# One product per chunk for dV and the transpose of P, in a backward pass of two attention blocks

## The chip, the cores and the metric

The kernel runs on one core of a Trainium2 chip. The metric is the device time of one execution in microseconds, and the median of three runs counts. The profile is of one further execution, taken by the hardware profiler.

## The reference

Two independent attention blocks, A and B, read caches of keys and values. Each has an input x of 8 batches x 96 tokens x 640, 32 heads of width 128, and 512 cached keys and values per batch and head. The reference returns the forward output of both and the gradients of all ten inputs, in bfloat16:

```
q = (x @ wq) per head;  scores = q k^T * 128^-0.5;  P = softmax(scores)
O = P v;  out = concat_heads(O) @ wo;  result = concat(out_A, out_B)
then the gradients of x, k_cache, v_cache, wq, wo for a given grad_out
```

Per head and batch (a "chunk" below: 64 heads x 8 batches = 512 of them) the backward pass needs dV = P^T dO, dP = dO V^T, delta = the row sums of O * dO, dS = (dP - delta) * P, dK = dS^T Q and dQ = dS K.

## The kernel before

An emitter collects pieces of code with a tick and a slot and writes them out in that order; one tick starts one chunk, and each stage of a chunk has a tick of its own (`OFF`). The tile framework then schedules the instructions of each engine by its own costs, hands out buffers and sets the semaphores. So eight chunks are in flight, and in a tick PE goes, after the head work of the tick before, through:

- S = Q K^T of the chunk that is 3 ticks old (L301, 96x512); DVE takes the negative row maximum `negm` (L303), ACT the exponential with its row sums (L313), DVE the reciprocal `rinv` (L323), POOL the scaling to `P_sb` (L332);
- `c_s8`: the dQ product of the oldest chunk (L343) and the four transposes of dS (L349), which DVE copies to `dST_sb` (L351); `c_s7`: dK (L435), evacuated by ACT (L438);
- `c_s45`: the O product (L362) and the four transposes of P (L368, P as the stationary operand and a 96-column identity as the moving one). O^T, dQ^T and P^T share one PSUM bank, `x_ps`; ACT evacuates O^T and dQ^T together to `OD` (L378) and then P^T to `PT_sb` (L381), which the O product of the next tick reads;
- `c_s4`: dV (L392, the same stationary chunks of P with 128 columns of dO as the moving operand) in a bank of its own, `dV_ps`, evacuated by ACT (L395);
- `c_s6`: dP (L420) in a bank, and the delta sum (L422), a product of `prod` with a column of ones, in another bank, `dl_ps`. `prod` = O * dO is POOL's work (L410). DVE computes `dS_sb` from both banks and `P_sb` (L424).

Around these lies the work per head and per group of heads: projections (L246), transposes of Q and dO to token-major form in `pD` (L261; the copies of both, `Qnat_h` and `dOnat_h`, are DVE's, L163), the products for dwo and dwq (L472, L493), and out and dx (L517). All products take their bank from one pool of eight, `ps`, in turn:

```
        def bank(shape, dt, name):
            return ps.tile(shape, dt, name=name, tag="bank")
```

The order in which the pieces of a tick are written, by slot: S, then `c_s8`, `c_s7`, `c_s45` (slot S5), `c_s4` (S4), `c_s6` (S6), and the head and group work. Loads, transposing loads and stores are DMAs on SP's queue.

Of the kernel before, what the change touches and what calls it, by code (L numbers as in the profile page):

```python
# [7 lines left out]
ACT = mybir.ActivationFunctionType  # L8
ALU = mybir.AluOpType
AX = mybir.AxisListType  # L10
F32 = mybir.dt.float32
BF16 = mybir.dt.bfloat16
PSUM = bass.MemoryType.PSUM
# [33 lines left out]
OFF = dict(ldk=-5, ldv=-4, kt=-3, vt=0, s2=3, s3=3, s4=4, s5=5, s6=6, s7=7, s8=8)  # L47
HK = dict(pA=-10, pA2=-9, pB=-3, pC0=[-2, 0], pC1=[-1, 0], pD1=1, pD0=2, qA0=18, qA1=17, qA1e=21, qDw=(18, 29), qB=[19, 20], qD=[(18, 0, 2), (19, 2, 4), (21, 4, 5)])
EV = dict(pB0="act", pB1="dve", pC00="act", pC01="act", pC10="act", pC11="dve", pD0="dve", pD1="dve", qA0="act", qA1="dve", qB0="act", qB1="dve", qD="dve", gU="act")
# [4 lines left out]
SLOTS = dict(LOAD=0, S2A=5, S2B=5.5, S1=6, S8=10, S7=20, S5=30, S4=40, S6=50, S3A=52, S3B=53, S5B=54, HEAD=SL_HEAD, GRP=SL_GRP)  # L54


def build_block(tc, em, tick0, blk, x, kc, vc, wq, wo, g_all, out_all, dx, dk, dv, dwq, dwo, ident, ones, pools, HG=6, first=True, groups=None):
    nc = tc.nc
    B, Sq, D = x.shape
    _, H, Sk, Dh = kc.shape  # L60
# [5 lines left out]
    KC = Sk // 128  # L66
    NB = 2
    assert B % NB == 0 and H % 2 == 0
    scale = float(Dh) ** -0.5
# [9 lines left out]
    while t0 < T:  # L79
        w = 512 if T - t0 >= 512 else (256 if T - t0 >= 256 else (128 if T - t0 >= 128 else T - t0))  # L80
# [4 lines left out]
    while c0 < D:  # L85
        w = 512 if D - c0 >= 512 else (256 if D - c0 >= 256 else 128)
# [12 lines left out]
    const, ps, kvp, wk, hd, hst, grp = (pools[k] for k in ("const", "ps", "kvp", "wk", "hd", "hst", "grp"))  # L99

    def bank(shape, dt, name):
        return ps.tile(shape, dt, name=name, tag="bank")
# [3 lines left out]
    SB = {}  # L106
    HS = pools["HS"]
    CS = pools["CS"]
# [49 lines left out]
    def evac(eng, dst, src, sc=None):  # L158
        if eng == "act":
            nc.scalar.activation(dst, src, ACT.Identity, scale=(1.0 if sc is None else sc))  # L160
        else:
            if sc is None:
                nc.vector.tensor_copy(dst, src)  # L163
            else:
                nc.vector.tensor_scalar(dst, src, float(sc), None, op0=ALU.mult)
# [84 lines left out]
    def pD(h, which):  # L250
        def f():
            st = HS[(blk, h)]
            src = st["QT_h"] if which == 0 else st["dOT_h"]
            dst = hd.tile([Sq, B * 128], BF16, name="Qnat_h" if which == 0 else "dOnat_h")
            st["Qnat_h" if which == 0 else "dOnat_h"] = dst
            for b0 in range(0, B, 8):
                nb = min(8, B - b0)
                n_ps = bank([Sq, 8 * 128], BF16, "n_ps")
                for i in range(nb):
                    b = b0 + i  # L260
                    nc.tensor.transpose(n_ps[:, i * 128:(i + 1) * 128], src[:, b * Sq:(b + 1) * Sq], ident[:])  # L261
                evac(EV["pD%d" % which], dst[:, b0 * 128:(b0 + nb) * 128], n_ps[:, 0:nb * 128])
        return f

    def c_ld(h, b, n, bufs):
# [89 lines left out]
    def c_s45(tick, k8, k5, k4):  # L355
        def f():
            pt_ps = XP.pop(tick)
            if k5 is not None:
                st = CS[(k5[0], k5[1], k5[2])]
                OT_ps = pt_ps[:, 0:2 * Sq].bitcast(F32)  # L360
                for c in range(KC):
                    nc.tensor.matmul(OT_ps, st["V_sb"][:, c, :], st["PT_sb"][:, c * Sq:(c + 1) * Sq], start=(c == 0), stop=(c == KC - 1))  # L362
            if k4 is not None:
                st4 = CS[(k4[0], k4[1], k4[2])]
                P_sb = st4["P_sb"]
                PT_ps = pt_ps[:, 4 * Sq:4 * Sq + KC * Sq]
                for c in range(KC):
                    nc.tensor.transpose(PT_ps[:, c * Sq:(c + 1) * Sq], P_sb[:, c * 128:(c + 1) * 128], ident[0:Sq, 0:Sq])  # L368
            both = [(k, which) for which, k in enumerate((k5, k8)) if k is not None]
            if both:  # L370
                at = [(HS[(k[0], k[1])]["slot"], k[2] * Sq) for k, _ in both]
                v = OD[:, both[0][1], at[0][0], at[0][1]:at[0][1] + Sq]
                src = pt_ps[:, 2 * Sq * both[0][1]:2 * Sq * (both[-1][1] + 1)].bitcast(F32)
                if len(both) == 2:
                    step = (OD.shape[2] + at[1][0] - at[0][0]) * T + at[1][1] - at[0][1]
                    v = bass.AP(v.tensor, v.offset, [v.ap[0], (step, 2), (1, Sq)])
                    src = src.rearrange("p (a q) -> p a q", a=2)
                nc.scalar.activation(v, src, ACT.Identity, scale=1.0)  # L378
            if k4 is not None:
                PT_sb = wk.tile([128, KC * Sq], BF16, name="PT_sb", bufs=2)  # L380
                nc.scalar.activation(PT_sb[:], PT_ps, ACT.Identity, scale=1.0)  # L381
                st4["PT_sb"] = PT_sb
        return f

    def c_s4(h, b):
        def f():
            st = CS[(blk, h, b)]
            hs = HS[(blk, h)]
            P_sb = st["P_sb"]
            dV_ps = bank([128, KC * 128], F32, "dV_ps")  # L390
            for c in range(KC):
                nc.tensor.matmul(dV_ps[:, c * 128:(c + 1) * 128], P_sb[:, c * 128:(c + 1) * 128], hs["dOnat_h"][:, b * 128:(b + 1) * 128], start=True, stop=True)  # L392
            if b % 2 == 0:
                SB[(blk, h, b // 2, "v")] = wk.tile([128, 2, KC * 128], BF16, name="dV_sb", bufs=4)
            nc.scalar.activation(SB[(blk, h, b // 2, "v")][:, b % 2], dV_ps[:], ACT.Identity, scale=1.0)  # L395
        return f

    def c_st(h, b, which):
# [5 lines left out]
    def c_s5b(h, b):  # L404
# [6 lines left out]
            st["prod"] = prod  # L411
        return f

    def c_s6(h, b):
        def f():
            st = CS[(blk, h, b)]
            hs = HS[(blk, h)]
            tok = slice(b * Sq, (b + 1) * Sq)
            dP_ps = bank([Sq, Sk], F32, "dP_ps")
            nc.tensor.matmul(dP_ps[:], hs["dOT_h"][:, tok], st["VT"], start=True, stop=True)  # L420
            dl_ps = bank([Sq, 1], F32, "dl_ps")
            nc.tensor.matmul(dl_ps[:], st["prod"][:], ones[:, 0:1], start=True, stop=True)  # L422
            dS_sb = wk.tile([Sq, Sk], BF16, name="dS_sb", bufs=2)
            nc.vector.scalar_tensor_tensor(dS_sb[:], dP_ps[:], dl_ps[:, 0:1], st["P_sb"][:], op0=ALU.subtract, op1=ALU.mult)  # L424
            st["dS_sb"] = dS_sb
        return f
# [136 lines left out]
    for g in range(NG):  # L563
        h0 = GH0[g]
        for hh in range(groups[g]):
            h = h0 + hh
# [16 lines left out]
            for b in range(B):  # L583
                ct = c0t + b
                if b % NB == 0:
                    em.add(tick0 - 12 if first and h == 0 and b == 0 else ct + OFF["ldk"], SLOTS["LOAD"], c_ld(h, b, "K", 7))
                    em.add(ct + OFF["ldv"], SLOTS["LOAD"], c_ld(h, b, "V", 6))
                    if not k_on_pe(h, b):
                        em.add(ct + OFF["kt"], SLOTS["LOAD"] + 1, c_xt(h, b, "KT", 4))
                    em.add(ct + OFF["vt"], SLOTS["LOAD"] + 1, c_xt(h, b, "VT", 4))  # L590
                if k_on_pe(h, b):
                    em.add(ct + 2, SLOTS["S1"], c_s1(h, b), pe=223)
                em.add(ct + OFF["s2"], SLOTS["S2A"], c_s2a(h, b))
                em.add(ct + OFF["s2"], SLOTS["S2B"], c_s2b(h, b))
                em.add(ct + OFF["s3"], SLOTS["S3A"], c_s3a(h, b))
                em.add(ct + OFF["s3"], SLOTS["S3B"], c_s3b(h, b))
                em.add(ct + OFF["s5"], SLOTS["S5B"], c_s5b(h, b))
                if b % 2 == 1:
                    em.add(ct + OFF["s4"] + 1, SLOTS["LOAD"] + 1.5, c_st(h, b, "v"))
                    em.add(ct + OFF["s7"] + 1, SLOTS["LOAD"] + 1.5, c_st(h, b, "k"))  # L600
                em.add(ct + OFF["s4"], SLOTS["S4"], c_s4(h, b))
                for i, o in enumerate(("s8", "s7", "s5", "s4")):
                    SX.setdefault(ct + OFF[o], [None] * 4)[i] = (blk, h, b)
                em.add(ct + OFF["s6"], SLOTS["S6"], c_s6(h, b))
                em.add(ct + OFF["s7"], SLOTS["S7"], c_s7(h, b))
            hk = HK if first or h < H - 1 else dict(HK, qA0=13, qB=[14, 15], qA1=16, qD=[(19, 0, 2), (19, 2, 4), (19, 4, 5)])
# [42 lines left out]
def _kernel_impl(tc, A_x, A_k_cache, A_v_cache, A_wq, A_wo, B_x, B_k_cache, B_v_cache, B_wq, B_wo, grad_out,  # L649
           out_0, out_1, out_2, out_3, out_4, out_5, out_6, out_7, out_8, out_9, out_10, HG=5, slots=None, off=None, hk=None, ev=None, gspread=None, groupsA=None, groupsB=(5, 5, 5, 5, 5, 5, 2)):  # L650
    global GSPREAD0, GSPREAD1
    nc = tc.nc
# [10 lines left out]
    with ExitStack() as ctx:  # L663
        P = lambda **kw: ctx.enter_context(tc.tile_pool(**kw))
        cst = P(name="gconst", bufs=1)
        ident = cst.tile([128, 128], BF16, name="ident")
# [4 lines left out]
        nc.vector.memset(warm[:], 1.0)  # L671
        pools = dict(
            const=P(name="const", bufs=1),
            ps=P(name="ps", bufs=8, space=PSUM),
            kvp=P(name="kv", bufs=11),
            wk=P(name="wk", bufs=3),
            hd=P(name="hd", bufs=2),
# [7 lines left out]
        pools["SX"] = {}  # L685
        pools["XP"] = {}
        pools["OD"] = pools["const"].tile([128, 2, HG + 2, A_x.shape[0] * A_x.shape[1]], BF16, name="OD", bufs=1)
        pools["HS"] = {}
        pools["CS"] = {}
        em = Emitter()  # L690
# [77 lines left out]
```

## Time and profile before

| | |
|---|---|
| time, median of three runs | 1630.79 us (1629.3 to 1632.03) |
| the profiled execution | 1629.74 us, span 1628.0 us |
| granted TensorE clock | 0.999 |
| DMA | 454.96 MB, mean 279 GB/s |

In a row of the profile's groups the line is that of the kernel above, then come engine, operation, what is written and read with shapes and count; behind the first bar the busy time in us and the mean of one in ns; behind the second the engine's idle time just before them, in us, and what ended it. In the waits a row reads: engine and work that waited, what it waited for, us in total, times, longest us. In the timeline a row gives start and duration in us; several equal instructions in a row are one line, with their count. Products overlap: the duration of one is its latency, and the distance between starts is what it costs PE.

### The profile page before, as it was taken

What the parts mean: (1) busy time and instruction counts of PE and PEld (TensorE: products, weight loads), DVE (VectorE), ACT (ScalarE), POOL (GpSimd) and SP (SyncE); (2) the same over time, 40 slices, a digit from 0 to 9 for tenths busy, and PEclk for the clock granted to TensorE, in tenths of its full rate; (3) what the DMA queues carried; (4) which work ended last, traced back from release to release, by engine and by line L of the source; (5) the groups of instructions that cost most, each with busy time, mean ns of one, the idle gap of its engine ahead of it and who ended that gap; (6) DMA issues with size and microseconds to landing.
All of it is one profiled execution on the core that took longest, in us unless ns stands there. A gap on an engine that the chain in (4) does not pass through costs nothing.

```text
span 1628.0 us, 55048 instructions
## 1 busy us (share of the span) xinstructions
PE 1605.0 (99%) x20881; PEld 1286.4 (79%) x21048; DVE 1269.9 (78%) x2907; ACT 1391.5 (85%) x3518; POOL 528.5 (32%) x1034
## 2 busy tenths in 40 slices
PE   8999999999999999999999999999999999999998
PEld 7887787787788787877878777877877877877876
DVE  6886687778788788788878767878878878777887
ACT  7999898798898797988879889978987977987984
POOL 2333333233333233333323323323333333332332
PEclk9999999999999999999999999999999999999999
DMA  9999999999999999999999999999999999999994
GB/s 268 284 290 293 274 292 285 278 275 289 283 281 287 274 282 278 272 277 299 277 303 287 285 285 286 283 294 277 276 295 268 294 288 266 283 274 285 287 280 142
DMA packets 875626, 454.96 MB, mean 279 GB/s; under 512 B 548192, under 2 KB 875360, under 8 KB 875360
## 3 DMA queue, kind: packets, MB, share of 16 engines
q1 hardware_dynamic: 875360, 451.43, 112.8%
q8 instruction: 165, 2.70, 0.7%
q14 instruction: 101, 0.83, 0.1%
HBM read 161.09 MB, written 159.12 MB: 197 GB/s over the span
## 4 chain that ended last, share of the span: by engine, by line
PE 93%; DVE 2%; ACT 2%; issue 1%; DMA 1%; SPq 0%; POOL 0%; DVEq 0%; ACTq 0%; POOLq 0%
PE q_ps L246 13%; PE o_ps L517 12%; PE dK_ps L435 7%; PE dV_ps L392 7%; PE dP_ps L420 7%; PE S_ps L301 7%; PE dwo_ps L472 6%; PE dwq_ps L493 6%; PE dst_ps L349 5%; PE x_ps L368 5%; PE x_ps L362 5%; PE x_ps L343 5%; PE n_ps L261 3%; PE nat_ps L458 3%; PE woT_ps L213 1%
## 5 line engine op out<-in xcount | busy, mean ns | idle before, releaser
L332 POOL TENSOR_SCALAR P_sb<-E_sb,rinv 96x512 bf16<-96x512 bf16 x512 | 354.2, 692 | 1072.2 <-DVE rinv L323 1038.4
L313 ACT ACTIVATE E_sb<-S_ps,negm 96x512 bf16<-96x512 f32 x512 | 356.3, 696 | 117.2 <-DVE negm L303 111.7
L424 DVE SCALAR_TENSOR_TENSOR dS_sb<-dP_ps,dl_ps,P_sb 96x512 bf16<-96x512 f32 x512 | 382.8, 748 | 43.6 <-PE dl_ps L422 36.6
L438 ACT ACTIVATE dK_sb<-dK_ps 128x512 bf16<-128x512 f32 x512 | 307.4, 600 | 84.8 <-PE dK_ps L435 83.8
L303 DVE TENSOR_REDUCE negm<-S_ps 96x1 f32<-96x512 f32 x512 | 347.6, 679 | 37.5 <-PE S_ps L301 36.4
L395 ACT ACTIVATE dV_sb<-dV_ps 128x512 bf16<-128x512 f32 x512 | 316.2, 618 | 0.0
L381 ACT ACTIVATE PT_sb<-x_ps 128x384 bf16<-128x384 bf16 x512 | 258.1, 504 | 0.0
L517 PEld LDWEIGHTS <-OD 128*128 128x128 bf16 x1536 | 135.3, 98 | 102.8 <-issue 2.0
L392 PE MATMUL dV_ps<-dOnat_h,P_sb 96*128 96x128 bf16 x2048 | 197.9, 219 | 0.6 <-DVE dOnat_h L163 0.6
L435 PE MATMUL dK_ps<-Qnat_h,dS_sb 96*128 96x128 bf16 x2048 | 198.0, 219 | 0.0
L420 PE MATMUL dP_ps<-VT,dOT_h 128*96 128x512 bf16 x512 | 195.3, 381 | 0.3
L323 DVE RECIPROCAL rinv<-rowsum 96x1 f32<-96x1 f32 x512 | 80.3, 157 | 144.8 <-ACT E_sb L313 141.5
L351 DVE COPY dST_sb<-dst_ps 128x384 bf16<-128x384 bf16 x512 | 177.7, 347 | 17.5 <-PE dst_ps L349 17.5
L410 POOL TENSOR_TENSOR prod<-OD,dOT_h 128x96 bf16<-128x96 bf16 x512 | 186.5, 364 | 8.8 <-ACT OD L378 8.2
L301 PE MATMUL S_ps<-KT,QT_h 128*96 128x512 bf16 x488 | 184.9, 379 | 0.4
L378 ACT ACTIVATE OD<-x_ps 128x192 bf16<-128x192 f32 (+1 forms) x515 | 173.3, 336 | 3.7 <-PE x_ps L343 3.7
L349 PE MATMUL dst_ps<-ident,dS_sb 96*128 96x96 bf16 x2048 | 172.4, 206 | 0.5 <-ACT PT_sb L381 0.3
L362 PE MATMUL x_ps<-PT_sb,V_sb 128*128 128x96 bf16 x2048 | 172.2, 206 | 0.2 <-ACT PT_sb L381 0.2
L368 PE MATMUL x_ps<-ident,P_sb 96*128 96x96 bf16 x2048 | 171.9, 205 | 0.6 <-POOL P_sb L332 0.3
L343 PE MATMUL x_ps<-dST_sb,K_sb 128*128 128x96 bf16 x2048 | 170.9, 206 | 0.0
L343 PEld LDWEIGHTS <-K_sb 128*128 128x128 bf16 x2048 | 135.3, 98 | 38.2
L493 PE MATMUL dwq_ps<-dQnat,x_nat 128*128 128x256 bf16 x960 | 142.7, 273 | 0.0
(75 smaller groups left out, 3042.5 us busy)
## 6 DMA issues: line engine op xcount, KB each, us to landing
out_dram<-dV_sb SPq DMA_DIRECT2D x256, 256.0 KB, 3.6
out_dram<-dK_sb SPq DMA_DIRECT2D x256, 256.0 KB, 3.5
K_sb<-in_A_k_cache_dram SPq DMA_DIRECT2D x128, 256.0 KB, 4.1
V_sb<-in_A_v_cache_dram SPq DMA_DIRECT2D x128, 256.0 KB, 3.9
K_sb<-in_B_k_cache_dram SPq DMA_DIRECT2D x128, 256.0 KB, 4.0
V_sb<-in_B_v_cache_dram SPq DMA_DIRECT2D x128, 256.0 KB, 4.0
out_dram<-dwo_sb SPq DMA_DIRECT2D x64, 160.0 KB, 3.2
out_dram<-dwq_sb SPq DMA_DIRECT2D x32, 320.0 KB, 4.2
```

What stands on the lines that cost most here:

```text
L301: nc.tensor.matmul(S_ps[:], hs["QT_h"][:, tok], st["KT"], start=True, stop=True)
L303: nc.vector.tensor_reduce(negm[:], S_ps[:], axis=AX.X, op=ALU.max, negate=True)
L313: nc.scalar.activation(E_sb[:], st["S_ps"][:], ACT.Exp, bias=st["negm"][:], scale=1.0, accum_out=rowsum[:])
L332: pinned(nc.gpsimd.tensor_scalar(P_sb[:], st["E_sb"][:], st["rinv"][:], 0.0, op0=ALU.mult, op1=ALU.add))
L343: nc.tensor.matmul(dQT_ps, st["K_sb"][:, c, :], st["dST_sb"][:, c * Sq:(c + 1) * Sq], start=(c == 0), stop=(c == KC - 1))
L392: nc.tensor.matmul(dV_ps[:, c * 128:(c + 1) * 128], P_sb[:, c * 128:(c + 1) * 128], hs["dOnat_h"][:, b * 128:(b + 1) * 128], start=True, s ...
L395: nc.scalar.activation(SB[(blk, h, b // 2, "v")][:, b % 2], dV_ps[:], ACT.Identity, scale=1.0)
L420: nc.tensor.matmul(dP_ps[:], hs["dOT_h"][:, tok], st["VT"], start=True, stop=True)
L424: nc.vector.scalar_tensor_tensor(dS_sb[:], dP_ps[:], dl_ps[:, 0:1], st["P_sb"][:], op0=ALU.subtract, op1=ALU.mult)
L435: nc.tensor.matmul(dK_ps[:, c * 128:(c + 1) * 128], dS_sb[:, c * 128:(c + 1) * 128], hs["Qnat_h"][:, b * 128:(b + 1) * 128], start=True, s ...
L438: nc.scalar.activation(SB[(blk, h, b // 2, "k")][:, b % 2], dK_ps[:], ACT.Identity, scale=1.0)
L517: nc.tensor.matmul(o_ps[:], src[:, t * 128:(t + 1) * 128], rhs, start=(hh == 0), stop=(hh == groups[g] - 1))
```

## The change

The four transposes of P and the four dV products of a chunk become four products with the same stationary chunk of P and 224 moving columns: 128 of dO and a 96-column identity, side by side. For this the token-major dO lies in a constant tile `DN`, double buffered by head, in which each pair of batches shares one identity: dO, identity, dO. The identities are written once at the start. The result goes into a pair of PSUM banks, `wide`, of a pool of its own with one buffer; two chunks of 224 f32 columns lie in each bank. ACT evacuates P^T (now f32) and then dV from it. The delta sum, `c_dl`, is issued just before that product, and goes to the last column of the second bank of the same tick's pair. The pool of single banks shrinks from eight to six.

```diff
@@ pD @@
+            if which == 0:
+                dst = hd.tile([Sq, B * 128], BF16, name="Qnat_h")
+                st["Qnat_h"] = dst
+            else:
+                dst = st["DN_h"] = pools["DN"][:, (blk * H + h) % 2]
...
+                    v = dst[:, b0 // 2, 0:128]
+                    v = bass.AP(v.tensor, v.offset, [v.ap[0], (128 * 2 + Sq, nb // 2), (128 + Sq, 2), (1, 128)])
+                    evac(EV["pD1"], v, n_ps[:, 0:nb * 128].rearrange("p (a b d) -> p a b d", b=2, d=128))
@@ c_s45 @@
-                PT_ps = pt_ps[:, 4 * Sq:4 * Sq + KC * Sq]
-                for c in range(KC):
-                    nc.tensor.transpose(PT_ps[:, c * Sq:(c + 1) * Sq], P_sb[:, c * 128:(c + 1) * 128], ident[0:Sq, 0:Sq])
...
-                PT_sb = wk.tile([128, KC * Sq], BF16, name="PT_sb", bufs=2)
-                nc.scalar.activation(PT_sb[:], PT_ps, ACT.Identity, scale=1.0)
@@ c_s4 @@
-            dV_ps = bank([128, KC * 128], F32, "dV_ps")
+            W = 128 + Sq
+            dV_ps = wide(tick)
+            rhs = hs["DN_h"][:, b // 2, (b % 2) * 128:(b % 2) * 128 + W]
             for c in range(KC):
-                nc.tensor.matmul(dV_ps[:, c * 128:(c + 1) * 128], P_sb[:, c * 128:(c + 1) * 128], hs["dOnat_h"][:, b * 128:(b + 1) * 128], start=True, stop=True)
+                nc.tensor.matmul(dV_ps[:, c // 2, (c % 2) * W:(c % 2 + 1) * W], P_sb[:, c * 128:(c + 1) * 128], rhs, start=True, stop=True)
+            both = dV_ps[:, :, 0:2 * W].rearrange("p a (c w) -> p a c w", w=W)
+            o_dv, o_pt = (0, 128) if b % 2 == 0 else (Sq, 0)
+            PT_sb = wk.tile([128, KC * Sq], BF16, name="PT_sb", bufs=2)
+            nc.scalar.activation(PT_sb[:].rearrange("p (a c q) -> p a c q", a=2, c=2), both[:, :, :, o_pt:o_pt + Sq], ACT.Identity, scale=1.0)
+            st["PT_sb"] = PT_sb
...
-            nc.scalar.activation(SB[(blk, h, b // 2, "v")][:, b % 2], dV_ps[:], ACT.Identity, scale=1.0)
+            nc.scalar.activation(SB[(blk, h, b // 2, "v")][:, b % 2].rearrange("p (a c d) -> p a c d", a=2, c=2), both[:, :, :, o_dv:o_dv + 128], ACT.Identity, scale=1.0)
@@ new @@
+    def wide(tick):
+        if tick not in pools["WP"]:
+            pools["WP"][tick] = pools["psw"].tile([128, 2, 512], F32, name="dV_ps", tag="wide")
+        return pools["WP"][tick]
+
+    def c_dl(h, b, tick):
+        def f():
+            st = CS[(blk, h, b)]
+            st["dl_ps"] = wide(tick)[0:Sq, 1, 511:512]
+            nc.tensor.matmul(st["dl_ps"], st["prod"][:], ones[:, 0:1], start=True, stop=True)
+        return f
@@ c_s6 @@
-            dl_ps = bank([Sq, 1], F32, "dl_ps")
-            nc.tensor.matmul(dl_ps[:], st["prod"][:], ones[:, 0:1], start=True, stop=True)
+            dl_ps = st["dl_ps"]
@@ the ticks @@
-                em.add(ct + OFF["s4"], SLOTS["S4"], c_s4(h, b))
+                em.add(ct + OFF["s4"], SLOTS["S4"], c_s4(h, b, ct + OFF["s4"]))
+                em.add(ct + OFF["s6"], SLOTS["S4"] - 1, c_dl(h, b, ct + OFF["s6"]))
@@ the pools @@
-            ps=P(name="ps", bufs=8, space=PSUM),
+            ps=P(name="ps", bufs=6, space=PSUM),
+            psw=P(name="psw", bufs=1, space=PSUM),
...
+        pools["DN"] = pools["const"].tile([Sqn, 2, Bn // 2, 2 * 128 + Sqn], BF16, name="DN", bufs=1)
+        for i in range(2):
+            for j in range(Bn // 2):
+                nc.gpsimd.tensor_copy(pools["DN"][:, i, j, 128:128 + Sqn], ident[0:Sqn, 0:Sqn])
```

More of the change, by code (lines that the diff above doesn't have):

```diff
@@ L253, in f @@
             src = st["QT_h"] if which == 0 else st["dOT_h"]
-            dst = hd.tile([Sq, B * 128], BF16, name="Qnat_h" if which == 0 else "dOnat_h")
-            st["Qnat_h" if which == 0 else "dOnat_h"] = dst
+            if which == 0:
[3 more added lines that the diff above has]
+                dst = st["DN_h"] = pools["DN"][:, (blk * H + h) % 2]
             for b0 in range(0, B, 8):
@@ L261, in f @@
                     nc.tensor.transpose(n_ps[:, i * 128:(i + 1) * 128], src[:, b * Sq:(b + 1) * Sq], ident[:])
-                evac(EV["pD%d" % which], dst[:, b0 * 128:(b0 + nb) * 128], n_ps[:, 0:nb * 128])
+                if which == 0:
+                    evac(EV["pD0"], dst[:, b0 * 128:(b0 + nb) * 128], n_ps[:, 0:nb * 128])
+                else:
+                    v = dst[:, b0 // 2, 0:128]
+                    v = bass.AP(v.tensor, v.offset, [v.ap[0], (128 * 2 + Sq, nb // 2), (128 + Sq, 2), (1, 128)])
+                    evac(EV["pD1"], v, n_ps[:, 0:nb * 128].rearrange("p (a b d) -> p a b d", b=2, d=128))
         return f
@@ L362, in f @@
                     nc.tensor.matmul(OT_ps, st["V_sb"][:, c, :], st["PT_sb"][:, c * Sq:(c + 1) * Sq], start=(c == 0), stop=(c == KC - 1))
-            if k4 is not None:
-                st4 = CS[(k4[0], k4[1], k4[2])]
-                P_sb = st4["P_sb"]
-                PT_ps = pt_ps[:, 4 * Sq:4 * Sq + KC * Sq]
-                for c in range(KC):
-                    nc.tensor.transpose(PT_ps[:, c * Sq:(c + 1) * Sq], P_sb[:, c * 128:(c + 1) * 128], ident[0:Sq, 0:Sq])
             both = [(k, which) for which, k in enumerate((k5, k8)) if k is not None]
@@ L378, in f, with c_s4 @@
                 nc.scalar.activation(v, src, ACT.Identity, scale=1.0)
-            if k4 is not None:
-                PT_sb = wk.tile([128, KC * Sq], BF16, name="PT_sb", bufs=2)
-                nc.scalar.activation(PT_sb[:], PT_ps, ACT.Identity, scale=1.0)
-                st4["PT_sb"] = PT_sb
         return f
-    def c_s4(h, b):
+    def c_s4(h, b, tick):
         def f():
@@ L687, in _kernel_impl @@
         pools["OD"] = pools["const"].tile([128, 2, HG + 2, A_x.shape[0] * A_x.shape[1]], BF16, name="OD", bufs=1)
+        Bn, Sqn = A_x.shape[0], A_x.shape[1]
+        assert Bn % 2 == 0 and 2 * (128 + Sqn) <= 512
+        pools["DN"] = pools["const"].tile([Sqn, 2, Bn // 2, 2 * 128 + Sqn], BF16, name="DN", bufs=1)
+        for i in range(2):
+            for j in range(Bn // 2):
+                nc.gpsimd.tensor_copy(pools["DN"][:, i, j, 128:128 + Sqn], ident[0:Sqn, 0:Sqn])
+        pools["WP"] = {}
         pools["HS"] = {}
```

## The prediction, made before the changed kernel ran

> **What bounds the kernel now.** I read the page first. Its busy shares and the chain that ended last both say TensorE:
>
> ```profile
> PE 1605.0 (99%) x20881; PEld 1286.4 (79%) x21048; DVE 1269.9 (78%) x2907; ACT 1391.5 (85%) x3518; POOL 528.5 (32%) x1034
> PE 93%; DVE 2%; ACT 2%; issue 1%; DMA 1%; SPq 0%; POOL 0%; DVEq 0%; ACTq 0%; POOLq 0%
> ```
>
> The reader is to see that PE has only 23 us of the span without work, and that ACT at 85% is next: a change that saves PE columns gains, and one that makes PE wait for ACT each tick loses. Then the groups, for the durations of the touched operations:
>
> ```profile
> L424 DVE SCALAR_TENSOR_TENSOR dS_sb<-dP_ps,dl_ps,P_sb 96x512 bf16<-96x512 f32 x512 | 382.8, 748 | 43.6 <-PE dl_ps L422 36.6
> L303 DVE TENSOR_REDUCE negm<-S_ps 96x1 f32<-96x512 f32 x512 | 347.6, 679 | 37.5 <-PE S_ps L301 36.4
> L395 ACT ACTIVATE dV_sb<-dV_ps 128x512 bf16<-128x512 f32 x512 | 316.2, 618 | 0.0
> L381 ACT ACTIVATE PT_sb<-x_ps 128x384 bf16<-128x384 bf16 x512 | 258.1, 504 | 0.0
> ```
>
> The 0.0 on both ACT rows says that ACT never idles before them: when it reaches the P^T and dV evacuations, their data has long been there. ACT runs behind PE, and today nobody pays for it. Then the waits: what dS waits for now is small, 36.6 us in 140 of 512 ticks, all of it PE.
>
> ```profile
> DVE dS_sb L424 <- PE dl_ps L422: 36.6, 140, 1.1
> ```
>
> Last the timeline of one tick (start, us, engine, operation), whose order decides the case:
>
> ```profile
> 804.65 0.34 PE L368 MATMUL x_ps<-ident,P_sb 96*128 96x96 bf16 x4
> 804.82 0.39 PE L392 MATMUL dV_ps<-dOnat_h,P_sb 96*128 96x128 bf16 x4
> 804.85 0.58 ACT L438 ACTIVATE dK_sb<-dK_ps 128x512 bf16<-128x512 f32 x1
> ...
> 805.04 0.38 PE L420 MATMUL dP_ps<-VT,dOT_h 128*96 128x512 bf16 x1
> ...
> 805.26 0.17 PE L422 MATMUL dl_ps<-ones,prod 128*96 128x1 bf16 x1
> ...
> 805.33 0.32 ACT L378 ACTIVATE OD<-x_ps 128x192 bf16<-128x192 f32 x1
> 805.50 0.75 DVE L424 SCALAR_TENSOR_TENSOR dS_sb<-dP_ps,dl_ps,P_sb 96x512 bf16<-96x512 f32 x1
> 805.54 0.49 ACT L381 ACTIVATE PT_sb<-x_ps 128x384 bf16<-128x384 bf16 x1
> ...
> 805.91 0.60 ACT L395 ACTIVATE dV_sb<-dV_ps 128x512 bf16<-128x512 f32 x1
> ...
> 807.18 0.34 PE L349 MATMUL dst_ps<-ident,dS_sb 96*128 96x96 bf16 x4
> ```
>
> dS runs 805.50 to 806.25 and PE needs it at 807.18; the dV evacuation ends only at 806.51. Over the trace dS starts a median 1.45 us before that evacuation ends, and ends a median 0.72 us before its transposes start.
>
> **The product, on PE.** Starts in the timeline give the pitch: four P^T products 0.17 us (43.4 ns each over all), four dV products 0.22 us (55.9 ns). The 256-column products of L493 follow at 109 ns, so 224 columns come to 55.9 + 96 x 0.416 = 96 ns. Per tick 4 x (43.4 + 55.9 - 96) = 13 ns saved, x512 = 7 us. The columns stay (96 + 128 = 224); what goes is the fixed part of 2048 products, and 2048 weight loads that PEld hides anyway. If the merged product has no such saving, it is 0.
>
> **Edits at nothing.** The delta sum keeps its 26 ns on PE (805.26 to 805.29); moved ahead of dV it needs prod some 0.6 us earlier, and in this tick prod (805.90 to 806.27, L410) is done 1 us before. The P^T evacuation now reads f32: the 320- and 512-element f32 evacuations take 453 and 600, so 384 lies near 502, against 504 now. The dO copy gets gaps in its output; the dQnat copy, which has them, takes 546 for 768 elements, on the line of the 677 for 1024. If the gaps cost what f32 costs (692 for 512), 64 x 0.7 = 45 us more on a DVE that is 22% idle. The eight identity copies on POOL are 96x96 each (its 128x128 MEMSET takes 205), under 2 us, before the first dV at 18 us. No DMA is added or moved; the dV stores on SP's queue follow their evacuation as before. PSUM: five banks a tick are taken from six instead of seven from eight, beside some 2.4 for head and group work, so a bank comes round after 0.81 tick instead of 0.85: nothing, while readers are not late.
>
> **The added wait.** The delta sum now sits in the second bank of the pair that ACT evacuates. In the changed program's order of instructions, 510 of the 512 dS operations wait for ACT's dV evacuation of the same tick (before: for PE, and DVE's own work). So a loop closes in each tick: dV evacuation, dS, transposes of dS, dK, delta sum, product, evacuations. In the trace of before the one bank that two engines read is S_ps, where exp needs negm's result anyway; a wait like the new one it does not show, so I bound the price.
>
> The Trainium skill (PSUM — Partial Sum Buffer, "PSUM bank collisions raise a hardware error") says that two engines may not touch one bank and quadrant at once, two reads included, and that accesses have to be kept apart per bank rather than per address. By that rule the wait can't be avoided as long as dl lies in this bank; no run here shows what happens without it.
>
> Behind the waiting dS on DVE are queued negm (which releases exp on ACT), rinv (which releases P on POOL) and the dS^T copy; for dS itself PE waits at the transposes, with everything behind them.
>
> The loop, from one product's start to the next, in rows: product 0.55 (three pitches of 0.096 and a last latency of about 0.26, between the 219 at 128 and 273 at 256 columns); hand-off to ACT 0.05; P^T start to dV evacuation end 0.97 (median); hand-off 0.04; dS 0.75; hand-off 0.06 (the shortest in the trace); transposes 0.17; dK 0.22; delta sum 0.03: 2.84 us, with ACT and DVE free in time. Ticks (from one dP to the next) now last 3.10 on average, but unevenly, since head work is uneven: 211 of 511 are under 2.85, and to lift those to 2.85 costs 55 us. That is the low end. The high end: had each dS of the trace waited for its evacuation, the transposes would be late in 429 ticks by 332 us together, if nothing were absorbed.
>
> Between them decides what DVE does around dS, by the changed order. In 249 ticks (mean 2.76 now) DVE takes the next tick's negm ahead of the waiting dS. S starts there a median 0.81 after the product; S 0.37, negm 0.68, dS 0.75, hand-off 0.06, transposes, dK, delta sum 0.42: 3.09. Tick by tick, with each one's own S, these ticks grow by 148 us. In the other 259 (mean 3.44) dS comes ahead of negm, and ACT's exp is late: 0.04 + dS 0.75 + negm 0.68 + 0.09 + exp 0.68 + dK and OD 0.69 (starts 804.85 to 805.54) + 0.97 = 3.90 from evacuation to evacuation. At 3.90 each these ticks would grow by 128 us; but PE feels it only where ACT's lateness reaches the next transposes, and longer ticks take it up. I take a floor of 3.2 for them, 24 us. Sum: 148 + 24 - 7 = 165 us.
>
> The profiled execution took 1629.74 (span 1628.0 and 1.7 around it), 1 us under the median of the three runs, 1630.79. 1630 + 165 = 1795. About 0.2%, 3 us, is what a measurement of this kernel can tell from no change.
>
> **Rivals.**
> - *Hidden wait, faster.* dS has 0.72 us of slack in the median and the changed PE order puts the O products ahead of the transposes in most ticks; with PE the bound, only the 7 us show: 1623. It decides if ACT, once PE slows at all, empties its queue so that evacuations end within 0.7 us of dS's present start. Against it: the loop alone is longer than 211 ticks. 5%.
> - *Bare loop.* Only ticks under 2.85 to 3.0 grow, 55 to 90 us, because the scheduler's DVE order costs nothing: 1630 + 55 - 7 = 1678, up to 1713. For it: ACT's idle time before exp (117 us) shows some room. 20%.
> - *Full chain through exp.* The late exp of the 259 ticks is not taken up: 148 + 128 - 7 = 269, 1899. For it: ACT at 85%, and no idle time before its evacuations. 15%.
> - *No change in the end*: waits that eat exactly the 7 us, 1630. 2%.
> - My forecast, 1715 to 1870: 55%. The other 3% lie above 1900 (six banks too few once readers are late, at the unabsorbed 332 us: 1955).
> That the product isn't merged can be left out: the changed PE order has 4096 loads and products fewer.
>
> The range 1675 to 1895 leaves out the hidden wait and the far end. Faster 0.05, same 0.02, slower 0.93.
>
> **What would show it.** Right: in the waits a large "DVE dS_sb <- ACT dV_sb"; PE busy well under 99% with waits of dst_ps on dS; idle time now before ACT's P^T evacuation; merged products at a pitch near 96 ns; exp waiting longer for negm. Wrong: dS starting within 0.1 us of the evacuation's end and still early for its transposes, PE at 99%; or a product pitch well over 100 ns, or dO copies over 1 us, which would move the cause.

## The result, and the profile after

The changed kernel takes 1878.2 us (three runs, 1878.0 to 1878.23) against 1630.79: 1.152 times, 95% interval 1.150 to 1.153, slower by 247 us. The forecast was 1795 with a range up to 1895. Its profiled execution took 1878.0, span 1875.9.

The page's busy times and the chain that ended last:

```profile
PE 1684.3 (90%) x19000; PEld 1272.1 (68%) x19000; DVE 1278.6 (68%) x2907; ACT 1431.0 (76%) x3518; POOL 527.7 (28%) x1042
PE 56%; DVE 21%; ACT 15%; issue 6%; DMA 1%; ACTq 0%; SPq 0%; DVEq 0%; POOL 0%
```

The chain was 93% PE; now DVE and ACT hold 36% of it, and the fullest engine, PE, is at 90% instead of 99%. The groups (line, engine, operation; busy us, mean ns; idle time before and what ended it):

```profile
L440 DVE SCALAR_TENSOR_TENSOR dS_sb<-dP_ps,dV_ps,P_sb 96x512 bf16<-96x512 f32 x512 | 382.9, 748 | 264.3 <-ACT dV_sb L400 221.7
L400 ACT ACTIVATE dV_sb<-dV_ps 128x512 bf16<-128x512 f32 x512 | 308.1, 602 | 0.0
L392 PE MATMUL dV_ps<-DN,P_sb 96*128 96x224 bf16 x2048 | 279.8, 257 | 0.3 <-DVE DN L163 0.3
L396 ACT ACTIVATE PT_sb<-dV_ps 128x384 bf16<-128x384 f32 x512 | 248.9, 486 | 1.8 <-PE dV_ps L392 1.0
```

The operations themselves cost what they were priced at: 486 ns for the f32 evacuation of P^T (502 forecast), 602 for dV (618 before). The merged products start 95 ns apart (median), as forecast. What is new is the idle time before dS. The waits show both ends of it:

```profile
DVE dS_sb L440 <- ACT dV_sb L400: 221.7, 216, 1.6
PEld L357 <- DVE dS_sb L440: 211.6, 305, 1.4
PE dst_ps L357 <- DVE dS_sb L440: 166.3, 290, 1.2
```

DVE stands at dS until ACT's dV evacuation has ended, and PE stands at the transposes until dS has. In 331 ticks dS starts within 0.1 us of the end of that evacuation (none before), and in 400 of 512 the transposes start within 0.08 us of the end of dS (28 before). In the waits of before, PE stood for dS once:

```profile
PE dst_ps L349 <- DVE dS_sb L424: 0.2, 1, 0.2
```

Two ticks of the timeline of after show the loop:

```profile
804.60 0.60 ACT L400 ACTIVATE dV_sb<-dV_ps 128x512 bf16<-128x512 f32 x1
...
805.24 0.75 DVE L440 SCALAR_TENSOR_TENSOR dS_sb<-dP_ps,dV_ps,P_sb 96x512 bf16<-96x512 f32 x1 [1.37 <-PE dwq_ps L509]
...
805.91 0.68 DVE L311 TENSOR_REDUCE negm<-S_ps 96x1 f32<-96x512 f32 x1
806.05 0.34 PE L357 MATMUL dst_ps<-ident,dS_sb 96*128 96x96 bf16 x4
...
806.65 0.54 PE L392 MATMUL dV_ps<-DN,P_sb 96*128 96x224 bf16 x4
806.68 0.68 ACT L321 ACTIVATE E_sb<-S_ps,negm 96x512 bf16<-96x512 f32 x1 [0.77 <-DVE negm L311]
...
807.36 0.58 ACT L454 ACTIVATE dK_sb<-dK_ps 128x512 bf16<-128x512 f32 x1
...
808.04 0.49 ACT L396 ACTIVATE PT_sb<-dV_ps 128x384 bf16<-128x384 f32 x1
...
808.41 0.60 ACT L400 ACTIVATE dV_sb<-dV_ps 128x512 bf16<-128x512 f32 x1
809.05 0.75 DVE L440 SCALAR_TENSOR_TENSOR dS_sb<-dP_ps,dV_ps,P_sb 96x512 bf16<-96x512 f32 x1 [0.30 <-ACT dV_sb L400]
...
809.86 0.34 PE L357 MATMUL dst_ps<-ident,dS_sb 96*128 96x96 bf16 x4 [0.82 <-DVE dS_sb L440]
```

The evacuation ends at 805.20 and dS starts at 805.24. (The mark behind dS names PE's dwq product, which ended at 805.22 and which dS does not read; so some of the idle time before dS stands under other names, and the 221.7 us for ACT are a lower bound.) The next tick's negm runs behind it, so exp starts only at 806.68, and ACT's dK, O and P^T work is late: the P^T evacuation starts at 808.04, though its product was done at 807.19. The dV evacuation ends at 809.01, 3.81 us after the one before (the forecast chain was 3.90). PE stands 0.82 us at the transposes. The lateness is made in the first tick and paid in the second.

### The profile page after: what moved, and what is told of

Its sections match the earlier page's. It is cut to its first block, busy times and chain, and to the rows that moved or that the text cites. A ratio compares the mean times of both kernels' runs of the same rounds, so it can differ in the third digit from the quotient of the medians.

```text
span 1875.9 us, 52031 instructions
## 1 busy us (share of the span) xinstructions
PE 1684.3 (90%) x19000; PEld 1272.1 (68%) x19000; DVE 1278.6 (68%) x2907; ACT 1431.0 (76%) x3518; POOL 527.7 (28%) x1042
## 4 chain that ended last, share of the span: by engine, by line
PE 56%; DVE 21%; ACT 15%; issue 6%; DMA 1%; ACTq 0%; SPq 0%; DVEq 0%; POOL 0%
DVE dS_sb L440 13%; PE dV_ps L392 9%; PE dst_ps L357 7%; PE o_ps L533 7%; PE q_ps L246 6%; PE dK_ps L451 6%; DVE negm L311 5%; PE dP_ps L437 4%; ACT dV_sb L400 4%; ACT PT_sb L396 3%; PE S_ps L309 3%; PE dwq_ps L509 3%; ACT E_sb L321 3%; ACT dK_sb L454 3%; PE n_ps L264 2%
## 5 line engine op out<-in xcount | busy, mean ns | idle before, releaser
L440 DVE SCALAR_TENSOR_TENSOR dS_sb<-dP_ps,dV_ps,P_sb 96x512 bf16<-96x512 f32 x512 | 382.9, 748 | 264.3 <-ACT dV_sb L400 221.7
L321 ACT ACTIVATE E_sb<-S_ps,negm 96x512 bf16<-96x512 f32 x512 | 349.2, 682 | 164.9 <-DVE negm L311 161.6
L454 ACT ACTIVATE dK_sb<-dK_ps 128x512 bf16<-128x512 f32 x512 | 303.1, 592 | 210.1 <-PE dK_ps L451 173.0
L400 ACT ACTIVATE dV_sb<-dV_ps 128x512 bf16<-128x512 f32 x512 | 308.1, 602 | 0.0
L392 PE MATMUL dV_ps<-DN,P_sb 96*128 96x224 bf16 x2048 | 279.8, 257 | 0.3 <-DVE DN L163 0.3
L357 PEld LDWEIGHTS <-dS_sb 96*128 96x128 bf16 x2048 | 105.5, 97 | 216.4 <-DVE dS_sb L440 211.6
L396 ACT ACTIVATE PT_sb<-dV_ps 128x384 bf16<-128x384 f32 x512 | 248.9, 486 | 1.8 <-PE dV_ps L392 1.0
L380 ACT ACTIVATE OD<-x_ps 128x192 bf16<-128x192 f32 (+1 forms) x515 | 165.6, 322 | 32.0 <-PE x_ps L370 14.5
L370 PE MATMUL x_ps<-PT_sb,V_sb 128*128 128x96 bf16 x2048 | 179.9, 206 | 2.6 <-ACT PT_sb L396 0.9
L392 PEld LDWEIGHTS <-P_sb 96*128 96x128 bf16 x2048 | 162.2, 97 | 0.6 <-issue 0.4
```

Of the source, the lines that this page charges most:

```text
L321: nc.scalar.activation(E_sb[:], st["S_ps"][:], ACT.Exp, bias=st["negm"][:], scale=1.0, accum_out=rowsum[:])
L357: nc.tensor.transpose(dST_ps[:, c * Sq:(c + 1) * Sq], st7["dS_sb"][:, c * 128:(c + 1) * 128], ident[0:Sq, 0:Sq])
L392: nc.tensor.matmul(dV_ps[:, c // 2, (c % 2) * W:(c % 2 + 1) * W], P_sb[:, c * 128:(c + 1) * 128], rhs, start=True, stop=True)
L396: nc.scalar.activation(PT_sb[:].rearrange("p (a c q) -> p a c q", a=2, c=2), both[:, :, :, o_pt:o_pt + Sq], ACT.Identity, scale=1.0)
L400: nc.scalar.activation(SB[(blk, h, b // 2, "v")][:, b % 2].rearrange("p (a c d) -> p a c d", a=2, c=2), both[:, :, :, o_dv:o_dv + 128], AC ...
L454: nc.scalar.activation(SB[(blk, h, b // 2, "k")][:, b % 2], dK_ps[:], ACT.Identity, scale=1.0)
```

## The experiments

The theory: the wait of dS for ACT's evacuations of the bank that the delta sum shares with dV and P^T is the loss. The rivals: six single banks instead of eight, or the merged product itself with its f32 and strided accesses. All times are medians, beside runs of the kernel before on the same chip (1629 to 1631).

**The delta sum in a bank of its own** (`own_bank`, on the changed kernel):

```diff
-            st["dl_ps"] = wide(tick)[0:Sq, 1, 511:512]
+            st["dl_ps"] = bank([Sq, 1], F32, "dl_ps")[:]
```

> The changed kernel with one edit: the delta sum goes to a single bank of its own from the pool of six, at the same place ahead of the product; merged product, pair, f32 evacuation and DN stay. Theory (the wait of dS for ACT's evacuations of the shared bank is the whole loss): dS no longer waits for ACT, PE is the bound again at 98 to 99% busy, and the 7 us of the merged product show: 1618 to 1632, against 1631 for the kernel before. Rival 1 (six single banks, the pair with one buffer, or the f32 and strided accesses cost the time): still over 1700, with no wait of dS for ACT. Rival 2 (both share): 1640 to 1700.

Measured: 1685.65, 1.034 times (1.033 to 1.036). So 192 of the 247 us go with one line, and 56 stay: rival 2. The line also changes the order that the framework writes: with the shared bank DVE takes the next tick's negm ahead of dS in 249 ticks, and PE the O products ahead of the transposes in 304; with a bank of its own it is none and 8, before none and 1. The 192 us are the wait together with the order made for it. What dS waits for, in this run's waits, is PE alone, and the transposes wait for nothing worth naming:

```profile
DVE dS_sb L440 <- PE dP_ps L437: 50.6, 145, 1.0
PE dst_ps L357 <- DVE dS_sb L440: 0.3, 1, 0.3
```

Its page has PE at 98% again, yet with more busy time than before, for fewer instructions:

```profile
PE 1654.8 (98%) x19000; PEld 1276.2 (76%) x19000; DVE 1283.7 (76%) x2907; ACT 1401.4 (83%) x3518; POOL 528.5 (31%) x1042
```

A product's duration is its latency, some 0.16 us longer than its share of PE (257 ns for the merged product, with 95 from start to start), so a wait of less than that between two products leaves no idle time. The starts show them. Undisturbed starts follow one another at 43.4 ns for 96 columns, 55.9 for 128, 95 for 224, 109 for 256 and 216 for 512, which 3.5 ns and 0.417 ns per column give within 2 ns; a start over 15 ns behind that is called late below. Here the delta sum is late in 112 ticks and dP in 118, 20 us each (before: under 1 us and 1.5 us), and what has just ended then is mostly a reader of some bank on ACT or DVE.

**The delta sum in the bank of the dS transposes** (`dst_bank`), which DVE alone reads:

```diff
-                dST_ps = bank([128, KC * Sq], BF16, "dst_ps")
+                dST_ps = dstb(tick)        # [128, 1024] bf16, one per tick
...
-            st["dl_ps"] = wide(tick)[0:Sq, 1, 511:512]
+            st["dl_ps"] = dstb(tick)[0:Sq, 1022:1024].bitcast(F32)
...
-                em.add(ct + OFF["s6"], SLOTS["S4"] - 1, c_dl(h, b, ct + OFF["s6"]))
+                em.add(ct + OFF["s6"], SLOTS["S8"] - 1, c_dl(h, b, ct + OFF["s6"]))
```

> The changed kernel with the delta sum in the bank of the dS transposes of the same tick, issued ahead of them; that bank is read by DVE only, so dS waits for no other engine, and a tick takes five single banks of six, not six of six. Theory (wait alone): 1618 to 1632 like the delta sum in a bank of its own. Rival (six banks are too few): faster than the bank of its own by 10 us or more. Possible price: POOL's prod is needed some 0.6 us earlier than in the changed kernel; if that shows, transposes of dS wait for POOL and the time is 1635 to 1680.

Measured: 1700.6, 1.043 times (1.042 to 1.045). The named price came, above its range: issued ahead of the transposes, the delta sum stops PE for POOL's prod.

```profile
PEld L433 <- POOL prod L415: 84.2, 207, 0.8
```

This run therefore says nothing on the banks.

**The shared bank alone** (`before_shared`, on the kernel before):

```diff
+                st6["dl_ps"] = pt_ps[0:Sq, 1022:1024].bitcast(F32)
+                nc.tensor.matmul(st6["dl_ps"], st6["prod"][:], ones[:, 0:1], start=True, stop=True)
...
-            dl_ps = bank([Sq, 1], F32, "dl_ps")
-            nc.tensor.matmul(dl_ps[:], st["prod"][:], ones[:, 0:1], start=True, stop=True)
+            dl_ps = st["dl_ps"]
```

> The kernel before with one part of the change alone: no merged product, eight banks, but the delta sum in the free last column of x_ps, the bank from which ACT evacuates O, dQ and the transpose of P; dS then waits for ACT's evacuation of the transpose. Theory (sharing a bank with ACT's evacuation is the cost by itself): slower, since dS starts about 0.5 us later than at present in a typical tick, and the chain from that evacuation through dS, negm, exp, dK and O back to it is 3.4 us against a mean tick of 3.1: 1670 to 1760, point 1720, less than the 1878 of the changed kernel because the 0.6 us dV evacuation is not in the chain. Rival (the merged product and the pair are the cost, not the shared bank): 1630 to 1640.

Measured: 1733.68, 1.064 times (1.062 to 1.065). No merged product, no pair, all eight banks: the place of a 96x1 sum costs 104 us by itself, through the same wait. The sum is also issued earlier here, ahead of dV; `before_dst` below, which issues it ahead of dV too but into a bank that ACT does not read, costs 3 us.

```profile
DVE dS_sb L427 <- ACT PT_sb L385: 172.5, 241, 1.4
```

**Seven and six banks** (`before_7banks`, `before_6banks`), one number each on the kernel before:

```diff
-            ps=P(name="ps", bufs=8, space=PSUM),
+            ps=P(name="ps", bufs=7, space=PSUM),
```

> The kernel before with seven single banks instead of eight, nothing else: 9.4 banks taken per tick out of seven, so a bank comes round after 0.74 tick; with the delta sum in a bank of its own the changed kernel had 8.4 out of six, 0.71 tick, and lost 56 us without any wait of dS for ACT. Theory (that rest is PE waiting for a bank whose reader on ACT or DVE is late): 1645 to 1690. Rival (the rest comes from the merged product, its pair with one buffer, or its evacuations): 1628 to 1636.

> The kernel before with six single banks, nothing else: a bank comes round after 6 / 9.4 = 0.64 tick. Runs so far by that measure: 0.85 (eight banks) 1630, 0.74 (seven) 1679, and with the merged product 0.81 1660, 0.71 1686. Theory (lack of banks is the rest of the loss, growing as the turn gets shorter): 1710 to 1800. Rival (seven banks met one bad turn and the rest is of the merged product): 1680 to 1700.

Measured: 1678.73 with seven (1.029, 1.028 to 1.031) and 1809.91 with six (1.111, 1.109 to 1.113). One bank less costs 48 us, two cost 180; the first is in the theory's range, the second 10 us above it. PE's weight loads come in the same order in all three kernels, so what differs on PE is waiting. With six the waits name what PE stands for, the evacuations that free the next bank in turn:

```profile
PE S_ps L301 <- ACT PT_sb L381: 8.0, 44, 0.3
PE q_ps L246 <- ACT PT_sb L381: 6.3, 18, 0.4
PE q_ps L246 <- ACT dK_sb L438: 4.2, 13, 0.3
PE S_ps L301 <- ACT dK_sb L438: 4.0, 25, 0.2
```

These are the visible ends of many short waits: by the distance between starts, S alone is late by 53 us in 223 ticks with six banks, 23 us in 127 with seven and 4 us in 44 with eight. The kernel before had no bank to spare.

**The evacuations bank by bank, with the delta sum in the first or the second** (`halves_dl0`, `halves_dl1`, on the changed kernel, the pair as two tiles of one bank):

```diff
+            for a in range(2):
+                nc.scalar.activation(pv[:, a], both[a][:, :, o_pt:o_pt + Sq], ACT.Identity, scale=1.0)
+                nc.scalar.activation(vv[:, a], both[a][:, :, o_dv:o_dv + 128], ACT.Identity, scale=1.0)
...
+            st["dl_ps"] = wide(tick)[0][0:Sq, 511:512]     # halves_dl1: wide(tick)[1]
```

> The changed kernel with the pair as two tiles of one bank each, evacuated bank by bank (P^T and dV of the first, then of the second: four ACT instructions, about 0.2 us more on ACT per tick), and the delta sum in the FIRST bank, so that dS waits for the first bank's dV only. Theory (the loop through the dV evacuation and dS sets the tick): the wait ends some 0.3 us sooner than in the changed kernel: 1740 to 1840, and at least 60 us below the same kernel with the delta sum in the second bank. Rival (ACT's load, not the wait, sets the time): 1890 to 1960 and equal to the other within 10 us.

> The same four evacuations bank by bank, the delta sum in the SECOND bank, so that dS waits for the last of them. Theory (loop): the evacuations take 0.2 us longer per tick than the two of the changed kernel, and the wait with them: 1890 to 1980. Rival (ACT's load): equal to the delta sum in the first bank within 10 us.

Measured: 1775.64 (1.089, 1.087 to 1.090) and 1850.24 (1.135, 1.133 to 1.136). The same four evacuations, and 75 us between them by the bank that the sum lies in, so these 75 us are not ACT's load. They stand where PE waits for dS, first with the sum in the first bank, then in the second:

```profile
PE dst_ps L357 <- DVE dS_sb L443: 49.4, 144, 1.0
PE dst_ps L357 <- DVE dS_sb L443: 127.5, 246, 1.1
```

By their starts the transposes are late by 101 and 187 us. The level of the second was missed; it is 28 us below the changed kernel, not above. In 278 ticks of its trace (200 with the sum in the first bank, 3 in the changed kernel) PE starts the merged product ahead of the transposes, so that ACT has the product before dS is needed; that this is the reason was not tried apart.

**Late in the bank of the transposes** (`dst_bank_late`): as `dst_bank`, but issued in the changed kernel's place, and DVE's copy of the transposes behind it.

> As the delta sum in the bank of the dS transposes, but issued where the changed kernel has it (ahead of the merged product, behind dK and O), and DVE's copy of the transposes issued behind it, so that POOL's prod has its time. Five single banks of six and no wait of dS for ACT. Theory (shared bank plus lack of banks are the whole loss, the merged product itself gains 7 us): 1618 to 1640. Rival (merged product and pair cost by themselves): 1660 to 1690, as the delta sum in its own bank.

Measured: 1660.0, 1.018 times (1.017 to 1.019), the lower edge of the rival's range. It is 26 us better than a bank of its own, and 29 us are left.

**The sum copied out of that bank** (`dst_bank_copied`), so that it is free before dS:

```diff
+            dl_sb = wk.tile([Sq, 1], F32, name="dl_sb", bufs=3)
+            nc.vector.tensor_copy(dl_sb[:], st["dl_ps"])
+            st["dl_ps"] = dl_sb
```

> As the delta sum late in the bank of the dS transposes, but DVE copies its 96x1 to SBUF right behind the copy of the transposes (some 0.16 us of DVE per tick, as rinv takes), so that this bank is free before dS runs and not after it. Theory (banks held long are what is left of the loss, 29 us): 1635 to 1655, below the 1660 without the copy. Rival (lack of banks is not it): 1660 or more, by the added DVE work.

Measured: 1664.56, 1.022 times (1.020 to 1.023). The rival's time, but not a clean answer: S is late by 6 us instead of 12 without the copy, while dK is late by 18 instead of 10 and the delta sum by 11 instead of 5. What an earlier free bank gains and what the added DVE work takes were not tried apart.

**The merged product with all eight banks in one pool** (`merged_8banks`): `dst_bank_late`, with the two halves of the pair taken from the common pool by `bank()`, `bufs=8`, and evacuated bank by bank.

> The merged product with all eight banks in one pool: its two halves are two single banks of it, evacuated bank by bank (four ACT instructions, some 0.2 us more on ACT per tick), the delta sum in the bank of the dS transposes, issued late as before. 9.4 banks out of eight, as in the kernel before. Theory (banks and the shared bank are the whole loss): back to 1620 to 1640, if ACT at some 90% keeps up; up to 1660 if it does not. Rival (the merged product and its evacuations cost by themselves): 1660 and more.

Measured: 1664.76, 1.022 times (1.021 to 1.024). Again the rival: with the turn of the kernel before (9.4 out of eight) and no wait of dS for ACT, 35 us are left. Two runs on the kernel before were to split them. **The evacuations of P^T and dV cut in two** (`before_split`):

```diff
+                for a in range(2):
+                    nc.scalar.activation(PT_sb[:, a * 2 * Sq:(a + 1) * 2 * Sq], PT_ps[:, a * 2 * Sq:(a + 1) * 2 * Sq], ACT.Identity, scale=1.0)
...
+            for a in range(2):
+                nc.scalar.activation(SB[(blk, h, b // 2, "v")][:, b % 2, a * 256:(a + 1) * 256], dV_ps[:, a * 256:(a + 1) * 256], ACT.Identity, scale=1.0)
```

> The kernel before with ACT's evacuations of P^T and of dV cut into two each (1024 more ACT instructions, some 0.2 us per tick), nothing else. It tells why the merged product with all eight banks in one pool still took 1665. Theory (ACT's added instructions release banks late, which is the 35 us left): 1650 to 1675. Rival (the merged product itself costs them): 1629 to 1637, since ACT has 15% of its time free.

Measured: 1642.6, 1.008 times (1.006 to 1.009): 12 us, between theory and rival. ACT was busy 50 us longer (1441.6 against 1391.5), 0.1 us per tick and not 0.2. **The delta sum's late place alone** (`before_dst`: `dstb`, `c_dl` and the copy behind it, nothing merged):

> The kernel before, unmerged, eight banks, with only the delta sum moved to the bank of the dS transposes, issued ahead of dV, and DVE's copy of the transposes behind it, as in the merged kernel with all eight banks (1665, of which 12 us went with the cut evacuations). 8.4 banks out of eight, so lack of banks is no more than in the kernel before. Theory (this place of the delta sum costs the rest, because DVE's copy waits for it): 1640 to 1655. Rival (the merged product or its f32 evacuation costs the rest): 1622 to 1634.

Measured: 1632.63, 1.0017 times (1.0009 to 1.0026): 3 us, the rival's number. If such costs added up, some 20 of the 35 us would be neither the cut evacuations nor the sum's place. The starts show that they do not add up. In `before_split` the transposes of dS are late, by 14 us (3 before); in `merged_8banks` they are late by 1 us, and S is late instead, by 26 us in 177 ticks (4 us in 44 before, 5 us in `before_split`, 7 us in `before_dst`). 163 of the 177 start within 0.08 us of the end of an exp, a dK or an O and dQ evacuation on ACT, and S reads the output of none of the three. So the larger part of the 35 us, some 22, is PE standing at S for a bank that ACT has not done with, though as many banks are taken per turn as in the kernel before. Why S meets banks here that ACT is late with is open. Since the two halves hold P^T in f32 beside dV, two banks are held until ACT's last evacuation, where x_ps held P^T in a bank that it needed anyway; that would fit, and no run takes it apart. No version that was run beats the kernel before.

## Why the prediction was right, and where its size was off

*The wait and its mechanism: right.* The order of instructions gave it away before any run: dS waits for the dV evacuation. The profile shows it as 221.7 us of DVE's time, and taking the sum out of the shared bank returns 192 us; the forecast for the wait was 148 + 24 = 172. The Trainium skill's rule (PSUM — Partial Sum Buffer, "PSUM bank collisions raise a hardware error") that two engines are kept apart by bank agrees with the traces: in each of the four runs in which ACT evacuates the sum's bank, no dS starts sooner than 0.03 us after the end of ACT's last read there. What happens without the wait was not tried.

*How the wait falls on the ticks: mis-sized.* The 249 ticks with negm ahead of dS went from 2.76 to 3.56 us, 199 us instead of 148; the other 259 from 3.44 to 3.62, 48 us instead of 24. The step that failed is "longer ticks take it up" and the floor of 3.2 that came from it. The late exp of a tick with dS first is paid by the next tick. The 143 ticks of the first kind that follow one of the second grow by 1.01 us each, 144.5 us together; there the dV evacuation ends a median 2.36 us after its product starts. The 105 that follow one of their own kind grow by 0.51 each; there it is 1.64 us. I had priced every one with ACT free in time, 1.57 us.

*PSUM at nothing: wrong, but hidden behind the wait.* "Nothing, while readers are not late" held 0.81 against 0.85 tick to be a small change. The kernel before loses 48 us with one bank less, and without the wait the changed kernel still takes 56 us more than before. In the changed kernel itself little of the 247 us is lack of banks. Its late starts come to 224 us at the transposes of dS (3 before), all but 1 us of it ended by dS; at S, dP and the delta sum, which are late by 50 us with a bank of its own for the sum, it is 14 us (6.5 before). That banks have time to come free while PE stands for dS would explain it; this reason is argued, not shown.

*The merged product: the pitch right, the gain not seen.* 95 ns per product against 43.4 + 55.9 is 4 ns less each, and no run turned the forecast 7 us into time. No version that merges was faster than 1660.

*A sign that did not come.* ACT has no idle time before the P^T evacuation (1.8 us); it idles ahead of dK instead (173.0 us for PE's product, 83.8 before), one step earlier in the same loop.

*The rest at nothing: right.* The copy into `DN` with its gaps takes 676 ns in the bank-of-its-own run (677 before), the f32 evacuation 486, the f32 and gapped dV evacuation 602.

*The rivals.* The hidden wait is refuted by the 400 ticks with transposes right behind dS, the bare loop (up to 1713) by the time. The full chain through exp (269, 1899) was nearer in size than the forecast: as the growth of the ticks shows, the chain's lateness is not taken up by long ticks but handed to short ones. The forecast's misses lie all on one side, so nothing cancelled: the time is 83 us above the point and only 17 us under the end of the range, and the range held by its width.

## What to carry to other kernels

Before a small result is put into the free corner of a PSUM bank, ask which engine reads the rest of that bank, and when: two readers on two engines turn one bank into a chain, and here a 96x1 sum cost 104 us where it cost 3 in a bank that its own reader evacuates. Where several short ticks follow long ones, price a loop from tick to tick, with the lateness that one hands to the next, not each tick by itself. Count how long banks are held against how often the pool comes round, before any bank is given away: a PE that is 99% busy does not show that it needs every one; here one bank less cost 48 us.

## What the runs showed of the hardware

Lack of banks hardly shows as idle time. With a bank of its own for the sum, PE was 98% busy, yet for 2048 fewer products than before it was busy 50 us longer, 1654.8 against 1605.0 (about 9 us of this are not real: the trace of before lacks the records of 167 of its 21048 products, and shows 9 us of idle time in gaps of under 0.06 us): waits shorter than a product's latency pass as work, and only the distance between starts tells. Late starts over all products, without the 512-column ones of q_ps and o_ps, some of which lack records, come to 29 us before, 85 with the bank of its own and 275 in the changed kernel: 56 and 246 us more, where the times are 56 and 247 us longer. The fall is steep: 0.85, 0.74 and 0.64 tick per turn of the pool gave 1630, 1679 and 1810 us.
